# Attention and FFN in one kernel: v of four loads by SyncE's queue with a cast on GpSimd, and five more transposes by DMA

## The chip, the cores and the metric

The kernel runs on one core of one Trainium2 chip. The metric is the device time of one execution in microseconds. The engines are named as in the profile: PE (TensorE), DVE (VectorE), ACT (ScalarE), POOL (GpSimd) and SP (SyncE, which issues DMAs only).

## The reference

Attention with a bias by bucket of distance, followed by a two-layer FFN on the heads put side by side. Batch 8, 8 heads, 576 positions, head dimension 64; FFN 512 to 2048 to 512. All inputs and the output are float32.

```python
scores = scale * np.matmul(q, k.transpose(0, 1, 3, 2))
scores = scores + bias.transpose(2, 0, 1)[None, :, :, :]      # bias_table[bucket(|i - j|)]
attn = np.exp(scores - np.max(scores, axis=-1, keepdims=True))
attn = attn / (np.sum(attn, axis=-1, keepdims=True) + 1e-09)
attn_out = np.matmul(attn, v)
x = attn_out.transpose(0, 2, 1, 3).reshape(B * S, H * D)
h = x @ w_in
out = np.maximum(0.01 * h, h) @ w_out
```

## The kernel before

The work is cut into 32 items, `items[n] = (b, p)`: batch b and pair p of heads (2p and 2p+1), four pairs to a batch. Item n is called pair n below, counted from 0. The order of the instructions on each engine is written out by hand; nothing is moved by a scheduler, and each engine and each DMA queue works in that order.

For each pair the kernel turns q and k so that the head dimension lies on the partitions (`transpose_q`, `transpose_k`, both done in the loop of the pair before). Up to pair 8 PE turns them, twelve small products per operand into PSUM (L275), and ACT or DVE copies the result out (L290, L294). From pair 9 on (`by_dma`) DVE first gathers the rows of both heads in a tile `pr` (`pair_rows`, L257), SP issues a DMA transpose of it into a tile `tu` (`turn_by_dma`, L265), and DVE copies from `tu` to `qt` and `kt`. `turn_ahead(n)` decides in which loop that is done: for the pairs up to 10 two loops ahead, later three.

`qk_mm` forms the scores in PSUM (L312, L315, L316 and, into the two banks `ps_q`, L305), `exp` writes the exponentials to `at` by ACT (L325, L328, L332), `band` multiplies a band of them by the exponential of the bias on DVE (L348). `av_tails` and `av` multiply with v (L361, L372); v has a column of ones, so the sum of the weights comes with it. DVE takes the reciprocal and writes `opair` (L375, L376). The banks of `av` and of `ps_q` are the same two, so L305 waits until `opair` is written. `x_transposes` then turns `opair` into `xT`: by PE and a copy (L394, L395), or for pairs that `x_by_dma` names by a DMA transpose that SP issues (L387).

The FFN works on blocks of 512 tokens as soon as the batches they need are finished: `ffn_in` (L420) and `leaky` write the hidden block `gt` (two buffers), `ffn_out` (L447) reads it. Its pieces are put between the steps of attention; what remains comes at the end (`moe_rest`).

Loads: q, k and v come in float32 and are cast to bf16 by the DMA itself, on POOL's queue: `load_qk`, `load_v_head`, `load_v_part` (one DMA per chunk of 128 positions, pieces of one head's 64 numbers), `load_v_tail` for the last 64 positions; the weights too (`load_w_in`, `load_w_out`, two halves each). q, k and v of a batch lie in one of two buffers (`qn`, `kn`, `vn`, by b % 2). Batch 0, half of q and k of batch 1 and the rest are issued ahead of the loop; `loads(n)`, called first in the loop of pair n through `begin(n)`, issues the others. In it a copy of one number of `opair` of pair n - 2 into `tick` holds POOL's queue back until that pair is done. SP's queue carries the bias tables `hk` at the start, then the DMA transposes and the stores of the output.

Of the kernel before, what the change touches and what calls it, by code (L numbers as in the profile page):

```python
# [10 lines left out]
FP32 = mybir.dt.float32  # L11
BF16 = mybir.dt.bfloat16
# [25 lines left out]
def kernel(  # L38
# [10 lines left out]
    nc = tc.nc  # L49

    B, H, S, D = q.shape
# [4 lines left out]
    P = 128  # L56
    n_pairs = H // 2
    NJ = S // P
# [3 lines left out]
    TT = 512  # L62
    n_tt = NT // TT
    n_fc = DF // P
# [11 lines left out]
    gt_pool = ctx.enter_context(tc.tile_pool(name="gt", bufs=2))  # L76
# [17 lines left out]
    NBUF = 2  # L94
# [4 lines left out]
    vn = [per.tile([P, NJ, H, D + 1], BF16, name=f"vn{i}") for i in range(NBUF)]  # L99
# [9 lines left out]
    def load_qk(b, h0, h1):  # L109
        i = b % NBUF  # L110
        for src, dst in ((q, qn[i]), (k, kn[i])):
            nc.gpsimd.dma_start(  # L112
                out=dst[0:RQ, h0:h1, :, :].rearrange("r h c d -> r h (c d)"),
                in_=src[b, h0:h1, :, :].rearrange("h (r c) d -> r h (c d)", c=NC),
            )

    def load_v_part(b, chunks, h0=0, h1=H):
        for c in chunks:
            nc.gpsimd.dma_start(  # L119
                out=vn[b % NBUF][:, c, h0:h1, 0:D],  # L120
                in_=v[b, h0:h1, c * P : (c + 1) * P, :].rearrange("h s d -> s h d"),
            )

    def load_v_head(b, h):
# [2 lines left out]
            in_=v[b, h, 0 : NJ * P, :].rearrange("(c s) d -> s c d", s=P),  # L127
        )

    def load_v_tail(b):  # L130
        for e in range(2):
            nc.gpsimd.dma_start(
                out=v4[b % NBUF][e * SL : (e + 1) * SL, :, 0:D],
                in_=v[b, e::2, NJ * P : S, :].rearrange("h s d -> s h d"),
            )

    def clear_v(eng, i):
        eng.memset(v4[i][:, :, D : D + 1], 1.0)
        eng.memset(vn[i][:, :, :, D : D + 1], 1.0)
# [39 lines left out]
    for j, (u, lo, w, m) in enumerate(groups):  # L179
        copy = nc.scalar.copy if j % 3 == 2 else nc.vector.tensor_copy  # L180
        copy(out=ub[:, C0 + lo : C0 + lo + m * w].rearrange("h (m w) -> h m w", w=w),
             in_=e8[:, u : u + m].unsqueeze(2).to_broadcast([H, m, w]))
    row = ub[:, :]
    nc.vector.tensor_copy(
        out=ub[:, C0 - BAND + 1 : C0],
        in_=bass.AP(tensor=row.tensor, offset=row.offset + C0 + BAND - 1,
                    ap=[list(row.ap[0]), [-1, BAND - 1]]),
# [3 lines left out]
    def load_hk(h0, h1):  # L191
        nc.sync.dma_start(
            out=hk[:, h0:h1, :],
            in_=bass.AP(tensor=udr, offset=h0 * UW, ap=[[1, P], [UW, h1 - h0], [1, BW]]),
        )

    def load_hk4(p0, p1):
        for e in range(2):
            nc.sync.dma_start(
                out=hk4[e * SL : (e + 1) * SL, p0:p1, :],  # L200
                in_=bass.AP(tensor=udr, offset=(2 * p0 + e) * UW + SL + P,
                            ap=[[1, SL], [2 * UW, p1 - p0], [1, P + SL]]),
            )
# [3 lines left out]
    load_hk(2, 4)  # L207
    load_hk4(1, n_pairs)
    load_hk(4, H)

    def mirrored(t, lo, hi):

        w = t.shape[-1]
        v = t[..., w - hi : w - lo]
        ap = [list(d) for d in v.ap]
        ap[-1][0] = -1
        return bass.AP(tensor=v.tensor, offset=v.offset + hi - lo - 1, ap=ap)
# [8 lines left out]
    load_v_head(0, 2)  # L226
    load_v_head(0, 3)
    load_qk(1, 0, H // 2)
    load_v_part(0, range(NJ), 4, H)
    clear_v(nc.gpsimd, 1)  # L230
    load_qk(1, H // 2, H)

    def load_w_in(half):
        o = slice(half * (DF // 2), (half + 1) * (DF // 2))
        nc.gpsimd.dma_start(out=w_in_sb[:, :, o], in_=moe_w_in[:, o].rearrange("(c p) f -> p c f", p=P))

    def load_w_out(half):
        n = n_fc // 2
        nc.gpsimd.dma_start(
            out=w_out_sb[:, half * n : (half + 1) * n, :],  # L240
            in_=moe_w_out[half * n * P : (half + 1) * n * P, :].rearrange("(f p) e -> p f e", p=P),
        )
# [3 lines left out]
    qts, kts, ops_ = {}, {}, {}  # L246
    N = len(items)
# [10 lines left out]
                                  in_=src[b % NBUF][0:RQ, 2 * p : 2 * p + 2, :, :].rearrange("r e c d -> r c e d"))  # L258

    def by_dma(n):  # L260
        return n > 2 * n_pairs

    def turn_by_dma(n):
        t = turned[n] = tu_pool.tile([P, 2 * NC, RQ], BF16, name="tu")
# [2 lines left out]
    def turned_pair(n, j):  # L267

        if by_dma(n):
            return turned[n][:, j * NC : (j + 1) * NC, :].rearrange("p c r -> p r c")  # L270
        ps = ps_m_pool.tile([P, 8 * P], BF16, name="ps_t", tag="m")
        b, p = items[n]
        for c in range(NC):
            for e in range(2):
                nc.tensor.transpose(ps[e * D : (e + 1) * D, c * RQ : (c + 1) * RQ],  # L275
                                    in_=(qn, kn)[j][b % NBUF][0:RQ, 2 * p + e, c, :],
                                    identity=ident[0:RQ, 0:RQ])
        return ps[:, 0:S].rearrange("p (c r) -> p r c", c=NC)
# [98 lines left out]
                                in1=rcp.to_broadcast([P, NJ + 1, D]), op=ALU.mult)  # L377

    def x_by_dma(n):
        return n_pairs + 2 <= n < N - 1 and n != 2 * n_pairs - 1  # L380

    def x_transposes(n):
        b, p = items[n]
        opair = ops_[n]
        w = (NJ + 1) * P
        if x_by_dma(n):
            nc.sync.dma_start_transpose(  # L387
                out=xT[p][:, b * S : b * S + w].rearrange("p (i t) -> p i t", t=P),
                in_=opair.rearrange("p i d -> p (i d)"),
            )  # L390
            return
        ps = ps_m_pool.tile([P, 8 * P], BF16, name="ps_tx", tag="m")
        for ic in range(NJ + 1):
            nc.tensor.transpose(ps[:, ic * P : (ic + 1) * P], in_=opair[:, ic, :], identity=ident)  # L394
        nc.vector.tensor_copy(out=xT[p][:, b * S : (b + 1) * S], in_=ps[:, 0:S])  # L395


    gts = {}
    rest = {"on": False, "turn": 0}

    def bank(name):

        if rest["on"]:
            turn = rest["turn"] = (rest["turn"] + 1) % 6
            if turn % 3 == 0:
                return ps_o_pool.tile([P, 512], FP32, name=name, tag=f"o{turn // 3}")
            if turn % 3 == 1:
                return ps_s_pool.tile([P, 512], FP32, name=name, tag="ps_s")
        return ps_m_pool.tile([P, 512], FP32, name=name, tag="m")

    def ffn_in(T, f, spare=None):
        if f == 0:
            gts[T] = gt_pool.tile([P, n_fc, TT], BF16, name="gt")
        t0 = T * TT
        if spare is None:
            pm = bank("pm1")
        else:
            pm = ps_o_pool.tile([P, 512], FP32, name="pm1", tag=f"o{spare}")
        for c in range(n_cc):
            nc.tensor.matmul(pm, lhsT=w_in_sb[:, c, f * P : (f + 1) * P], rhs=xT[c][:, t0 : t0 + TT],  # L420
                             start=(c == 0), stop=(c == n_cc - 1))
        return pm
# [61 lines left out]
    def step(kind):  # L484
        T, s = made[kind], at_piece[kind]
        at_piece[kind] = (s + 1) % n_fc
        if at_piece[kind] == 0:
            made[kind] += 1
        return T, s
# [5 lines left out]
    def piece_in(spare=None):  # L495
        T, s = step("in")
        leaky(T, s, ffn_in(T, s, spare))
# [107 lines left out]
    tick = per.tile([1, 1], BF16, name="tick")  # L605

    def loads(n):

        b, p = items[n]
        if n == 0:  # L610
            load_w_in(0)
            load_v_part(1, range(NJ))
            load_v_tail(1)
            load_w_in(1)
            load_w_out(0)
        elif n == 2:
            load_qk(2, 0, H // 2)
            load_w_out(1)
        if b < 1 or p < 1 or b > B - 2:
            return  # L620
        nc.gpsimd.tensor_copy(out=tick, in_=ops_[n - 2][0:1, 0, 0:1])  # L621
        if p == 1:
            load_qk(b + 1, H // 2, H)
            load_v_part(b + 1, (0,))
        elif p == 2:
            load_v_part(b + 1, (1, 2, 3))
        else:
            load_v_tail(b + 1)
            if b + 2 < B:
                load_qk(b + 2, 0, H // 2)  # L630

    def begin(n):
        loads(n)
        if by_dma(n + 1):
            turn_ahead(n)

    def turn_ahead(n):
        for m in range(n + 2, min(n + AHEAD + 1, N)):
            if by_dma(m) and m - (AHEAD if m > 2 * n_pairs + 2 else 2) == n:
                pair_rows(m)  # L640
                turn_by_dma(m)
# [47 lines left out]
    n = n_pairs  # L689
# [24 lines left out]
    for n in range(n_pairs + 1, N + 1):  # L714
        live = n < N
        more = n + 1 < N
        if x_by_dma(n - 2):
            finished(n - 2)
# [30 lines left out]
        if not x_by_dma(n - 1):  # L749
            finished(n - 1)  # L750
# [5 lines left out]
        if room["only"]:  # L756
            exp(n, 3, ps_b)
            moe(2)
            exp(n, 4, ps_c)
            score(n, 5)  # L760
            T, f = step("in")
            room["left"] -= 1

            def last_bands():
                band(n, 5)
                band(n, 4)

            leaky(T, f, ffn_in(T, f), True, last_bands)
            moe(room["left"])
            continue  # L770
# [44 lines left out]
```

## Time and profile before

| | us |
|---|---|
| median of 3 runs | 378.06 (377.69 to 379.08) |
| the profiled execution | 378.04 |
| its span, from the first to the last instruction | 376.3 |
| PE busy | 366.1 |
| ACT busy | 239.9 |
| DVE busy | 199.1 |
| POOL busy | 77.3 |

Busy time is the time in which an engine had an instruction in work. A row of the profile's groups gives the line, the engine, the operation, what is written and read, the shape and the count, then the busy us, the mean ns of one, and the idle time of the engine just before with what ended it. In a timeline the first number is the start in us from the beginning of the span and the second the duration; instructions of one kind that follow each other are merged. DMA rows give the count, the size of one and the us from issue to landing.

### The profile page before, as it was taken

What the parts mean: (1) busy time and instruction counts of PE and PEld (TensorE: products, weight loads), DVE (VectorE), ACT (ScalarE), POOL (GpSimd) and SP (SyncE); (2) the same over time, 40 slices, a digit from 0 to 9 for tenths busy, and PEclk for the clock granted to TensorE, in tenths of its full rate; (3) what the DMA queues carried; (4) which work ended last, traced back from release to release, by engine and by line L of the source; (5) the groups of instructions that cost most, each with busy time, mean ns of one, the idle gap of its engine ahead of it and who ended that gap; (6) DMA issues with size and microseconds to landing.
All of it is one profiled execution on the core that took longest, in us unless ns stands there. A gap on an engine that the chain in (4) does not pass through costs nothing.

```text
span 376.3 us, 8737 instructions
## 1 busy us (share of the span) xinstructions
PE 366.1 (97%) x3604; PEld 186.7 (50%) x3604; DVE 199.1 (53%) x502; ACT 239.9 (64%) x376; POOL 77.3 (21%) x118
## 2 busy tenths in 40 slices
PE   7879999999999999999999999999999999999996
PEld 3455555554555555555545545555555544444442
DVE  3678577777657666666755666655553300200221
ACT  5998886568856787777866666767777255055000
POOL 8763422333023303330323033100000000000000
PEclk9999999999999999999999999999999999999999
DMA  8999999998599959997998399453111000110212
GB/s 104 189 194 186 206 199 120 181 179 121 77 119 157 145 85 123 151 152 91 142 118 132 72 124 127 74 79 77 47 47 47 28 30 0 59 54 0 82 60 84
DMA packets 104351, 40.06 MB, mean 106 GB/s; under 512 B 83184, under 2 KB 98808, under 8 KB 104312
## 3 DMA queue, kind: packets, MB, share of 16 engines
q0 software_dynamic: 53696, 18.36, 47.2%
q1 hardware_dynamic: 50472, 21.02, 31.7%
q8 instruction: 28, 0.46, 0.5%
q10 hardware_dynamic: 144, 0.13, 0.1%
q14 instruction: 11, 0.09, 0.1%
HBM read 37.68 MB, written 9.45 MB: 125 GB/s over the span
## 4 chain that ended last, share of the span: by engine, by line
PE 89%; DMA 5%; POOL 2%; DVE 2%; ACT 1%; issue 1%; DVEq 0%; ACTq 0%; POOLq 0%
PE pm L447 34%; PE pm L420 32%; PE ps_o L372 10%; PE ps_s L312 8%; DMA vn<-in_v_dram 3%; PE ps_s L315 2%; DMA v<-in_v_dram 1%; PE ps_o L361 1%; PE ps_q L305 1%; DVE opair L376 1%; PE ps_tx L394 1%; PE ps_t L275 1%; ACT at L325 1%; POOL kn L112 1%; POOL qn L112 0%
## 5 line engine op out<-in xcount | busy, mean ns | idle before, releaser
L420 PE MATMUL pm<-xT,w_in_sb 128*128 128x512 bf16 x576 | 138.4, 379 | 0.1
L433 ACT ACTIVATE gt<-pm 128x512 bf16<-128x512 f32 x138 | 82.5, 603 | 86.2 <-PE pm L420 85.7
L447 PE MATMUL pm<-w_out_sb,gt 128*128 128x512 bf16 x576 | 132.5, 379 | 0.0
L325 ACT ACTIVATE at<-ps_s 128x1024 bf16<-128x1024 f32 x128 | 124.2, 1028 | 8.2 <-PE ps_s L312 8.1
L348 DVE TENSOR_TENSOR at<-at,hk 128x768 bf16<-128x768 bf16 (+3 forms) x160 | 71.0, 453 | 32.7 <-ACT at L328 19.9
L447 PEld LDWEIGHTS <-gt 128*128 128x128 bf16 x576 | 53.0, 98 | 60.6
L420 PEld LDWEIGHTS <-w_in_sb 128*128 128x128 bf16 x576 | 52.0, 98 | 54.8 <-issue 0.7
L465 DVE COPY y<-pm 128x512 f32<-128x512 f32 x33 | 22.8, 691 | 76.6 <-PE pm L447 76.6
L372 PE MATMUL ps_o<-vn,at 128*128 128x65 bf16 x1280 | 49.8, 194 | 0.4 <-DMA vn<-in_v_dram 0.4
L372 PEld LDWEIGHTS <-at 128*128 128x128 bf16 x1280 | 44.7, 97 | 9.5 <-issue 1.2
L312 PE MATMUL ps_s<-qt,kt 64*128 64x512 bf16 x256 | 40.1, 381 | 3.5 <-ACT at L325 3.0
L375 DVE RECIPROCAL rcp<-ps_o 128x5 f32<-128x5 f32 x64 | 12.3, 192 | 45.1 <-PE ps_o L372 45.1
L376 DVE TENSOR_TENSOR opair<-ps_o,rcp 128x320 bf16<-128x320 f32 x64 | 31.5, 492 | 3.3
L119 POOL DMA_DIRECT2D vn<-in_v_dram x32 | 29.6, 931 | 10.0 <-PE ps_s L312 5.6
L621 POOL COPY tick<-opair 1x1 bf16<-1x1 bf16 x18 | 4.7, 263 | 130.8 <-DVE opair L376 130.8
L312 PEld LDWEIGHTS <-kt 64*128 64x128 bf16 x256 | 8.4, 94 | 29.0 <-issue 21.5
L332 ACT ACTIVATE at<-ps_s 128x576 bf16<-128x576 f32 x32 | 21.8, 681 | 0.2 <-PE ps_s L316 0.2
L328 ACT ACTIVATE at<-ps_q 128x256 bf16<-128x256 f32 x64 | 21.5, 402 | 0.3 <-PE ps_q L305 0.2
L457 ACT COPY y<-pm 128x256 f32<-128x256 f32 x1 | 0.4, 372 | 27.5 <-DVE y L457 27.5
L294 DVE COPY kt<-tu 128x576 bf16<-128x576 bf16 x23 | 15.5, 674 | 0.0
L290 DVE COPY qt<-tu 128x576 bf16<-128x576 bf16 x23 | 15.0, 650 | 0.4 <-DMA tu<-pr 0.4
L112 POOL DMA_DIRECT2D qn<-in_q_dram x18 | 14.1, 782 | 4.2 <-PE ps_t L275 1.3
(57 smaller groups left out, 175.0 us busy)
## 6 DMA issues: line engine op xcount, KB each, us to landing
out_dram<-y SPq DMA_DIRECT2D x35, 256.0 KB, 2.3
qn<-in_q_dram POOLq DMA_DIRECT2D x14, 288.0 KB, 5.9
kn<-in_k_dram POOLq DMA_DIRECT2D x14, 288.0 KB, 7.1
vn<-in_v_dram POOLq DMA_DIRECT2D x28, 128.0 KB, 5.2
w_in_sb<-in_moe_w_in_dram POOLq DMA_DIRECT2D x2, 1024.0 KB, 12.9
w_out_sb<-in_moe_w_out_dram POOLq DMA_DIRECT2D x2, 1024.0 KB, 15.9
qn<-in_q_dram POOLq DMA_DIRECT2D x4, 144.0 KB, 4.3
kn<-in_k_dram POOLq DMA_DIRECT2D x4, 144.0 KB, 4.6
```

What stands on the lines that cost most here:

```text
L119: nc.gpsimd.dma_start(out=vn[b % NBUF][:, c, h0:h1, 0:D], in_=v[b, h0:h1, c * P : (c + 1) * P, :].rearrange("h s d -> s h d"),)
L312: nc.tensor.matmul(ps[:, e, :], lhsT=kt[r, u * P : (u + 1) * P], rhs=qt[r, 0:512], start=True, stop=True)
L325: nc.scalar.activation(at[:, :, u, 0:512], ps, AF.Exp, scale=scale)
L328: nc.scalar.activation(at[:, e, :, 512:S], ps[e][:, 0 : NJ * SL].rearrange("p (c i) -> p c i", i=SL), AF.Exp, scale=scale)
L332: nc.scalar.activation(at4[:, 0:S], ps.rearrange("p e i -> p (e i)")[:, 0:S], AF.Exp, scale=scale)
L348: nc.vector.tensor_tensor(out=o, in0=o, in1=m, op=ALU.mult)
L372: nc.tensor.matmul(ps[:, ic, :], lhsT=at[:, o : o + P], rhs=vn[b % NBUF][:, c, 2 * p + e, :], start=False, stop=(ic == NJ and c == NJ - 1))
L376: nc.vector.tensor_tensor(out=opair[:, :, e * D : (e + 1) * D], in0=ps[:, :, 0:D], in1=rcp.to_broadcast([P, NJ + 1, D]), op=ALU.mult)
L420: nc.tensor.matmul(pm, lhsT=w_in_sb[:, c, f * P : (f + 1) * P], rhs=xT[c][:, t0 : t0 + TT], start=(c == 0), stop=(c == n_cc - 1))
L433: nc.scalar.activation(g, pm, AF.Prelu, bias=0.0, scale=1.0, alpha=0.01)
L447: nc.tensor.matmul(pm, lhsT=gt[:, f, ts * P : (ts + 1) * P], rhs=w_out_sb[:, f, :], start=(f == 0), stop=(f == n_fc - 1))
L465: nc.vector.tensor_copy(out=y, in_=pm)
```

## The change

`stage`, a float32 tile that shares its two buffers with `gt`, takes v as it is by SP's queue (`stage_v`), and POOL casts it into `vn` (`cast_v`). This replaces the casting DMAs of POOL's queue for heads 4 to 7 of batch 0, for batch 1 and for batch 2 (in two halves, in the loops of pairs 5 and 6). For batch 1 it is done in the loop of pair 3; a copy of one number by DVE into `stage` holds SP's DMAs until `opair` of pair 1 is there, and `load_w_out(0)`, the first half of `load_qk(2)` and `load_w_out(1)` are issued behind the cast. For batch 2 POOL's one-number copy goes into `stage` instead of `tick`; the cast stands in the loop of pair 7.

`by_dma` begins at pair 7 instead of 9. By `turn_ahead`, pair 7's rows are gathered and turned in the loop of pair 5 behind its first band product, pair 8's at the start of the loop of pair 6. Where the next pair is turned by DMA, `band(n, 0)` stands ahead of `transpose_q(n + 1)`, which now holds for the loops of pairs 6 and 7 too. `x_by_dma` begins at pair 5 instead of 6.

```diff
+    stage = gt_pool.tile([P, 2 * NJ, H, D], FP32, name="stage", tag="gt")
+
+    def stage_v(b, chunks, h0=0, h1=H):
+        for c in chunks:
+            nc.sync.dma_start(
+                out=stage[:, c, h0:h1, :],
+                in_=v[b, h0:h1, c * P : (c + 1) * P, :].rearrange("h s d -> s h d"),
+            )
+
+    def cast_v(b, h0=0, h1=H):
+        for c in range(NJ):
+            nc.gpsimd.tensor_copy(out=vn[b % NBUF][:, c, h0:h1, 0:D], in_=stage[:, c, h0:h1, :])
...
     load_hk4(1, n_pairs)
     load_hk(4, H)
+    stage_v(0, range(NJ), 4, H)
...
     load_qk(1, 0, H // 2)
-    load_v_part(0, range(NJ), 4, H)
     clear_v(nc.gpsimd, 1)
     load_qk(1, H // 2, H)
+    cast_v(0, 4, H)
...
     def by_dma(n):
-        return n > 2 * n_pairs
+        return n > 2 * n_pairs - 2
...
     def x_by_dma(n):
-        return n_pairs + 2 <= n < N - 1 and n != 2 * n_pairs - 1
+        return n_pairs + 1 <= n < N - 1 and n != 2 * n_pairs - 1
...
-            gts[T] = gt_pool.tile([P, n_fc, TT], BF16, name="gt")
+            gts[T] = gt_pool.tile([P, n_fc, TT], BF16, name="gt", tag="gt")
...
         if n == 0:
             load_w_in(0)
-            load_v_part(1, range(NJ))
             load_v_tail(1)
             load_w_in(1)
+        elif n == 3:
+            nc.vector.tensor_copy(out=stage[0:1, 0, 0, 0:1], in_=ops_[n - 2][0:1, 0, 0:1])
+            stage_v(1, range(NJ))
+            cast_v(1)
             load_w_out(0)
-        elif n == 2:
             load_qk(2, 0, H // 2)
             load_w_out(1)
         if b < 1 or p < 1 or b > B - 2:
             return
-        nc.gpsimd.tensor_copy(out=tick, in_=ops_[n - 2][0:1, 0, 0:1])
+        done = ops_[n - 2][0:1, 0, 0:1]
+        if b == 1 and p < 3:
+            nc.gpsimd.tensor_copy(out=stage[0:1, 2 * p - 2, 0, 0:1], in_=done)
+            stage_v(b + 1, (2 * p - 2, 2 * p - 1))
+        else:
+            nc.gpsimd.tensor_copy(out=tick, in_=done)
         if p == 1:
             load_qk(b + 1, H // 2, H)
+        if p == 1 and b > 1:
             load_v_part(b + 1, (0,))
-        elif p == 2:
+        elif p == 2 and b > 1:
             load_v_part(b + 1, (1, 2, 3))
-        else:
+        elif p == 3:
+            if b == 1:
+                cast_v(b + 1)
             load_v_tail(b + 1)
```

## The prediction

> **What bounds the kernel now.** I read the page first, then busy time by stretch, then the chain of work that ended last, then DVE, POOL and the DMA landings around the pairs that change.
>
> ```profile
> span 376.3 us, 8737 instructions
> PE 366.1 (97%) x3604; PEld 186.7 (50%) x3604; DVE 199.1 (53%) x502; ACT 239.9 (64%) x376; POOL 77.3 (21%) x118
> DMA  8999999998599959997998399453111000110212
> ```
> ```profile
> 20.00:30.00 10.00, 8.42 (x179) 5.84 (x180) 7.49 (x21) 9.33 (x14) 6.35 (x9) 1.00 1.48 192
> 40.00:50.00 10.00, 10.00 (x150) 6.00 (x147) 7.07 (x18) 8.45 (x13) 4.08 (x6) 1.00 1.26 205
> 50.00:60.00 10.00, 10.00 (x150) 6.05 (x150) 7.75 (x20) 8.03 (x13) 2.96 (x5) 1.00 2.09 169
> ```
>
> The stretch rows give busy us of PE, PEld, DVE, ACT, POOL, then clock, DMA share and GB/s. PE is busy 366.1 of 376.3 us. In the first 30 us ACT leads (9.33 of 10 us against PE's 8.42); from 40 us on PE has no gap, so PE work that goes away there is worth its full time, provided nothing PE waits for comes late. The DMA row is the warning: nearly all nines for the first 40% of the span. The loads of the first three batches and the weights form one unbroken backlog, and the change moves things inside it. The profiled execution took 378.04 us, 1.74 more than its span and 0.02 from the median 378.06; sums are made against 378.04. About 0.5% (1.9 us) is what a measurement of this kernel can tell from no change.
>
> **What leaves PE.** The chain of waits, in order of time (start, us, what):
>
> ```profile
> 49.22 0.38 PE ps_t L275 x12
> 51.17 0.38 PE ps_t L275 x12
> 51.55 0.54 PE ps_s L312 x4
> 52.09 0.19 PE ps_q L305 x8
> 52.28 0.39 PE ps_tx L394 x5
> 57.90 0.38 PE ps_t L275 x12
> 59.86 0.38 PE ps_t L275 x12
> ```
>
> q and k of pairs 7 and 8 (counted from 0) are the four groups of twelve transposes, the output of pair 5 the group of five, all on the chain: 4 x 0.38 + 0.39 = 1.91 us. The order of the FFN's pieces doesn't depend on these flags, so nothing else of PE's program changes. **If nothing came late: 378.04 - 1.91 = 376.13.**
>
> **What DVE gives back.** Each turned pair costs two `pair_rows` copies on DVE, put at the start of pair 6 (for pair 8) and behind the first band product of pair 5 (for pair 7).
>
> ```profile
> L257 DVE COPY pr<-kn 96x768 bf16<-96x768 bf16 x1 | 0.3, 348 | 0.0
> PEld L305 <- DVE opair L376: 0.4, 2, 0.2
> 42.53 0.19 DVE L375 RECIPROCAL rcp<-ps_o 128x5 f32<-128x5 f32 x1 [0.24 <-PE ps_o L372]
> ```
> ```profile
> 48.18 0.68 DVE L431 TENSOR_TENSOR gt<-low,pm 128x512 bf16<-128x512 bf16 x1
> 49.26 0.20 DVE L375 RECIPROCAL rcp<-ps_o 128x5 f32<-128x5 f32 x1 [0.39 <-PE ps_o L372]
> 49.55 0.49 DVE L376 TENSOR_TENSOR opair<-ps_o,rcp 128x320 bf16<-128x320 f32 x1
> 49.96 0.75 DVE L290 COPY qt<-ps_t 128x576 bf16<-128x576 bf16 x1
> 50.63 0.41 DVE L348 TENSOR_TENSOR at<-at,hk 128x512 bf16<-128x512 bf16 x1
> 51.21 0.20 DVE L375 RECIPROCAL rcp<-ps_o 128x5 f32<-128x5 f32 x1 [0.17 <-PE ps_o L372]
> ```
>
> The wait row shows PE's `ps_q` products waiting, in both these pairs, for the `opair` of the head before (it empties their bank): no slack there. Two copies take about 0.62 us (0.35 each, overlapping slightly); in pair 5 DVE has 0.24 us idle ahead of the reciprocal, so 0.62 - 0.24 = 0.38 us reaches PE. In pair 6 the same 0.62 falls into 0.39 us idle; besides, the k transposes that covered the evacuation are gone: PE has only the 0.54 us of L312 between `av` and `ps_q`, and the evacuation takes about 0.2 + 0.49 + 0.17 = 0.86. I take 0.32 for both together. Bounds: 0 to 0.7 each. Pair 7 keeps an FFN piece at that place, 0. **Floor: 376.13 + 0.38 + 0.32 = 376.8.** Casts, slot and gate below are counted apart.
>
> **The step that decides: k of batch 2.** `pair_rows(8)` reads q and k of heads 0 to 3 of batch 2. Before, they were read on PE at 57.90. Now DVE reaches them at 48.18 + 0.68 = 48.86 and stands in order: behind it wait the evacuation of pair 5, the band products and the copy of qt. When did k land?
>
> ```profile
> 21.82 0.75 POOL L235 DMA_DIRECT2D w_in_sb<-in_moe_w_in_dram  x1 [1.72 <-DMA qn<-in_q_dram]
> 34.16 0.89 POOL L239 DMA_DIRECT2D w_out_sb<-in_moe_w_out_dram  x1 [4.22 <-DMA w_in_sb<-in_moe_w_in_dram]
> 36.91 0.67 POOL L112 DMA_DIRECT2D kn<-in_k_dram  x1 [0.35 <-DMA vn<-in_v_dram]
> ```
> ```profile
> w_in_sb<-in_moe_w_in_dram POOLq DMA_DIRECT2D x1, 1024.0 KB, 12.1
> kn<-in_k_dram POOLq DMA_DIRECT2D x1, 288.0 KB, 14.1
> vn<-in_v_dram POOLq DMA_DIRECT2D x4, 128.0 KB, 11.9
> ```
>
> Issued at 36.91, 14.1 us to landing: 51.0. That is already 2.1 us too late for 48.86, so the change must bring it forward. What moves it:
> - v off POOL's queue: 512 x 4 + 1024 x 4 = 6144 pieces leave it and go to SP's queue, same pieces, fp32 instead of bf16.
>
> ```profile
> DMA packets 2978, 0.49 MB, mean 165 GB/s; under 512 B 2924, under 2 KB 2924, under 8 KB 2977
> DMA packets 2003, 0.73 MB, mean 243 GB/s; under 512 B 1875, under 2 KB 1881, under 8 KB 2002
> ```
>
>  The first row is v alone (30 to 33 us): about 975 small packets per us, so 6.3 us of DMA. The nearest row of 256-byte packets on SP's queue is the second (67 to 70 us, transposes): 625 per us, 9.8 us. Uncast copies may as well be cheaper, down to half. I take the same 6.3, a shift of 0 (-3.1 to +3.5).
> - POOL waits ahead of `load_w_in(0)` for the half v of batch 0 to land and its four casts; before, it issued at 21.82. v's half was landing until 26.96 (below), so I put it at 28. The gap on POOL's queue is partly filled by v of batch 1 on SP's: +0.5 (0 to 2).
> - `load_w_out(0)`, and q and k behind it, wait for v of batch 1: gate on DVE at about 24.8, four issues, some 11.9 us as before, casts: 37 to 41 instead of 34.16. POOL's queue still holds w_in's second half then: 0 (0 to 2).
> - New beside it on SP's queue: two chunks of v of batch 2 and the turn of pair 7, 2048 + 1152 pieces, 3.3 us at 975 per us. A third of it ahead of k: +1.0 (0 to 3.3).
>
> So k lands at 51.0 + 0.5 + 1.0 = 52.5. From there DVE needs the k copy 0.35, evacuation 0.7, band 0.41, qt 0.65, evacuation 0.7: 2.8 us to `ps_q`, 55.3 against 51.92 before (+3.4; the earlier savings and losses are swallowed by the wait). Then 0.39 + 2 x 0.38 = 1.15 is still saved. **Sum: 378.04 + 3.4 - 1.15 = 380.3**; in general 378.04 + (landing - 50.3).
>
> The Trainium skill (DMA: Bandwidth & Descriptors, Issuing engines are not separate DMA queues) says that DMAs from SP, ACT and GpSimd run on the same 16 DMA engines and interleave, so that a second issuer saves sequencer time only. By that rule the shift of the first item is 0 and the sum stays 380.3; it speaks against the hope of 376. The shift of 0 itself was taken from the packet counts.
>
> **Small parts.**
>
> ```profile
> 26.96 0.67 PE L372 MATMUL ps_o<-vn,at 128*128 128x65 bf16 x17 [0.43 <-DMA vn<-in_v_dram]
> masks.py:197 POOL MEMSET ident<- 128x128 bf16 x1 | 0.2, 231 | 0.0
> L799 POOL MEMSET const-float32-0.0<- 128x1 f32 x1 | 0.1, 98 | 0.2 <-issue 0.2
> 7.66 0.41 SPq L192 DMA_DIRECT2D hk<-u_row  x1
> 11.78 0.67 SPq L192 DMA_DIRECT2D hk<-u_row  x1
> DMA to landing us min/median/max: 3.3/4.0/8.1
> ```
>
> No row shows a cast on POOL. From its memsets, (231 - 98) / 127 = 1.0 ns per element: 0.36 us for 256, 0.62 for 512; 4 x 0.36 + 8 x 0.62 = 6.4 us in place of twelve v issues at some 0.9. POOL is busy 21%, so only its order counts. v of batch 0: PE waited 0.43 us for it; without that wait -0.43, with the last cast behind a landing at 27 some +0.8. SP pays per issue 0.41 us for 256 pieces and 0.67 for 512, by that slope 1.2 for 1024; behind the stage loads stand the turns of pairs 7 and 8 and the output transpose of pair 5. w_in's first half landed at 33.9, first used at 34.67; if its issue slips to 28, PE may wait 0 to 4 us, swallowed by the later wait up to 3.4. The gate on DVE is one small copy of an `opair` that is there: 0.1, in the ACT-led stretch. The slot that `stage` takes from gt is free again in pair 7's loads; the second token block starts after pair 7's output: 0, and if v of batch 2 came 10 us late, a wait of that.
>
> **Rivals.**
> 1. *All in time, no loss.* If uncast pieces cost half (-3.1), k lands by 48.9 and v's 0.43 goes too: 376.8 - 0.43 = 376.4 with both give-backs, 375.7 with neither, **376.1** in the middle. For: 1.91 us of PE work is gone for certain, and 6144 pieces are out of POOL's queue. Against: 51.0 in an unbroken backlog, and two added waits of POOL. Chance 0.26.
> 2. *v of batch 1 starves* beside w_in's big packets, POOL stands behind its cast, and w_out, q and k are issued at 41 or later, behind an empty queue: k at 57, **384.7**. Decides when v of batch 1 lands after 40. Chance 0.17.
> 3. *The turns come late.* Pair 8's stands behind two chunks of v; with the longest landing of the rows, 8.1 us, plus 2 us of issue, about 59 against a need at 58: 1 to 3 us on top of the floor, **379**. Chance 0.07.
> 4. *Casts block DVE.* A two-input product (L348) waits for one cast in each of three bursts: 0.36 + 0.62 + 0.62 = 1.6 on the floor: **378.4**. No row shows a POOL compute beside DVE. Chance 0.05. The Trainium skill (SBUF — State Buffer, SBUF: two separate sides) has this rule: one port pair is locked for a whole instruction by a GpSimd operation or by a DVE operation with two SBUF inputs, and the other blocks; no run here shows it yet.
>
> **How the numbers follow.** Forecast 380.3, chance 0.45, with k at 50 to 54.5, 377.7 to 382.3. Of it 0.17 lies within 0.5% (below 379.9), 0.28 above. Rival 1 gives 0.17 faster (give-backs mostly hidden, below 376.1) and 0.09 same, rival 2 0.17 slower, rivals 3 and 4 0.05 same and 0.07 slower. Together: faster 0.17, same 0.31, slower 0.52. The range from 375.8 to 386.0 leaves out the last of both ends.
>
> **What would show it.** Right: PE 1.9 us less busy, 53 fewer PE instructions; DVE idle 2 to 4 us at L257 in pair 6, released by the DMA of kn, PE then idle at L305 for `opair`; w_out, q and k issued after 37. Wrong: no idle time at L257 (rival 1); POOL's first cast of batch 1 ending after 41 (rival 2); DVE idle at L290 on tu (rival 3); L348 longer beside casts (rival 4).

## The result, and the profile after

The changed kernel takes 397.77 us in the median of 6 runs (395.17 to 401.54), the kernel before 377.78 beside it. The ratio of the two, with the one slow run of 401.54 us left out, is 1.0505, interval 1.0463 to 1.0548. The forecast was 380.3 with a range to 386.0; the change costs 20.0 us where 2.3 were expected. The profiled execution took 395.67 us with a span of 393.9, so 17.6 us more than the span before. It is that difference which the rows explain.

The page of the changed kernel, span, busy time and the slices of PE, granted clock and DMA:

```profile
span 393.9 us, 8604 instructions
PE 365.5 (93%) x3497; PEld 187.0 (47%) x3551; DVE 200.6 (51%) x506; ACT 240.1 (61%) x376; POOL 72.6 (18%) x118
PE   7859960999999999999999999999999999999995
PEclk9996995799999999999999999999999999999999
DMA  9999999869966975999499939943111100110112
```

PE's weight loads fell from 3604 to 3551: the 53 transposes are gone. PE's busy time did not fall by their 1.9 us, and the clock row says why: it shows two dips, where the same work takes longer. The second of them, the 7th slice of PE, is a hole. The stretches give both places (busy us of PE, PEld, DVE, ACT, POOL, then clock, DMA share, GB/s):

```profile
20.00:30.00 10.00, 6.15 (x123) 4.28 (x123) 5.51 (x15) 7.45 (x11) 2.24 (x5) 0.94 1.02 179
30.00:40.00 10.00, 9.72 (x139) 6.26 (x137) 7.07 (x19) 7.24 (x10) 5.47 (x9) 0.72 1.15 206
60.00:70.00 10.00, 1.81 (x11) 0.82 (x12) 3.06 (x6) 0.00 (x0) 1.89 (x4) 0.50 1.29 185
```

From 60 to 70 us PE is busy 1.81 us and ACT not at all, while DMA moves 185 GB/s: everybody waits for a transfer. The waits of PE and DVE name it (engine, line, releaser: total us, times, longest):

```profile
PE ps_q L319 <- DVE opair L390: 12.1, 2, 11.7
PE ps_o L386 <- POOL vn L141: 2.8, 2, 2.2
DVE qt L304 <- DMA tu<-pr: 10.3, 1, 10.3
DVE pr L271 <- DMA kn<-in_k_dram: 1.4, 1, 1.4
```

And the chain of work that ended last, in order of time (start, us, what):

```profile
47.30 19.54 DMA tu<-pr
66.87 0.64 DVE qt L304
67.64 0.50 DVE opair L390
68.19 0.39 PE ps_q L319 x7
```

PE stands 11.7 us at the `ps_q` products of pair 6, because the `opair` that empties their bank is queued on DVE behind the copy of pair 7's q (`qt`, L304) out of the tile in which the DMA transpose lays its turned q and k, and that turn took 19.54 us. The k of batch 2, the forecast's deciding wait, shows as 1.4 us on DVE and 0.43 us on PE.

Landmarks on PE's timeline tell how much each wait carries to the end. First the kernel before, then the changed one, the same products in each: the first of `av` in the loop of pair 5, `ps_q` in the loop of pair 6, then both in the loop of pair 7. Ahead of them, in the changed kernel, stand the two waits for v of batch 0.

```profile
39.50 0.31 PE L361 MATMUL ps_o<-v,at 64*128 64x65 bf16 x10
...
51.92 0.35 PE L305 MATMUL ps_q<-qt,kt 64*128 64x64 bf16 x8
...
56.88 0.31 PE L361 MATMUL ps_o<-v,at 64*128 64x65 bf16 x10
...
61.58 0.28 PE L305 MATMUL ps_q<-qt,kt 64*128 64x64 bf16 x8
```
```profile
28.65 0.19 PE L386 MATMUL ps_o<-vn,at 128*128 128x65 bf16 x1 [2.20 <-POOL vn L141]
29.43 1.10 PE L386 MATMUL ps_o<-vn,at 128*128 128x65 bf16 x17 [0.59 <-POOL vn L141]
...
43.95 0.32 PE L375 MATMUL ps_o<-v,at 64*128 64x65 bf16 x10
...
56.32 0.20 PE L319 MATMUL ps_q<-qt,kt 64*128 64x64 bf16 x1 [0.43 <-DVE opair L390]
68.19 0.39 PE L319 MATMUL ps_q<-qt,kt 64*128 64x64 bf16 x7 [11.67 <-DVE opair L390]
...
75.04 0.31 PE L375 MATMUL ps_o<-v,at 64*128 64x65 bf16 x10
...
78.77 0.28 PE L319 MATMUL ps_q<-qt,kt 64*128 64x64 bf16 x8
```

PE is 4.45 us behind in pair 5 (v of batch 0 late by 2.20 and 0.59, then half clock), 4.40 at `ps_q` of pair 6, 16.1 when the wait of 11.67 is over, 18.2 at `av` of pair 7's loop and 17.2 at its `ps_q`; the span ends 17.6 later. So **11.7 us come from the turn of pair 7, 4.4 from the stretch before, 2.1 from half clock behind the wait (2.45, less the 0.39 of pair 5's transposes), and the stretch that has lost pair 8's transposes takes 1.0 off.** Of that 1.0 the rows of the transposes give 0.76; the 0.4 us that the span gains behind the last landmark were not traced.

Why does a turn take 19.5 us? Two rows of SP's own queue (start, us to issue, instruction), and the packets moved in two windows, 54 to 58 us and 30 to 31 us (packets, MB, time as a share of 16 engines; q0 is POOL's queue, q1 is SP's; the last row is SP's queue alone):

```profile
42.54 1.43 SPq L134 DMA_DIRECT2D stage<-in_v_dram  x2
47.30 10.24 SPq L279 DMA_TRANSPOSE tu<-pr  x1
```
```profile
q0 software_dynamic: 609, 0.61, 90.4%
q1 hardware_dynamic: 607, 0.16, 29.7%
```
```profile
q1 hardware_dynamic: 985, 0.25, 110.5%
```

Alone, SP's queue moved 985 small packets per us. Beside POOL's backlog of q, k and w_out it got one packet for each of POOL's, 607 against 609 in 4 us, or 152 per us, and POOL's are about 1 KB each (0.61 MB in 609). Between 20 and 24 us it was 773 against 775, 193 per us. Ahead of the turn in that queue stand two chunks of v, 2048 pieces, then its own 1152. At 152 to 193 per us these 3200 take 16.6 to 21.1 us; from v's issue at 42.54 to the turn's landing at 66.84 it was 24.3 us. The difference lies at the start: from 42 to 46 us SP's queue moved no packet at all, and from 46 to 47 only 45. From 46.4, when they begin in earnest, to the landing it is 20.4 us, or 157 per us for the 3200, which is the pace of one for one (in the last of these microseconds the queue already moves pieces of the next two chunks of v). Why nearly 4 us pass between the issue and the first packets, the record doesn't show.

### The profile page after: what moved, and what is told of

It is laid out like the page before. It is cut to its first block, busy times and chain, and to the rows that moved or that the text cites. A ratio compares the mean times of both kernels' runs of the same rounds, so it can differ in the third digit from the quotient of the medians.

```text
span 393.9 us, 8604 instructions
## 1 busy us (share of the span) xinstructions
PE 365.5 (93%) x3497; PEld 187.0 (47%) x3551; DVE 200.6 (51%) x506; ACT 240.1 (61%) x376; POOL 72.6 (18%) x118
## 4 chain that ended last, share of the span: by engine, by line
PE 78%; DMA 13%; SPq 2%; DVE 2%; ACT 1%; issue 1%; another core or an unknown queue 1%; POOL 0%; DVEq 0%; POOLq 0%
PE pm L461 31%; PE pm L434 28%; PE ps_o L386 9%; PE ps_s L326 7%; DMA stage<-in_v_dram 5%; DMA tu<-pr 5%; DMA kn<-in_k_dram 2%; PE ps_s L329 1%; PE ps_o L375 1%; SPq L134 1%; PE ps_q L319 1%; DMA u_row<-ub 1%; SPq L212 1%; DMA tabT<-in_bias_table_dram 1%
## 5 line engine op out<-in xcount | busy, mean ns | idle before, releaser
L461 PE MATMUL pm<-w_out_sb,gt 128*128 128x512 bf16 x556 | 130.8, 379 | 1.0
L461 PEld LDWEIGHTS <-gt 128*128 128x128 bf16 x576 | 53.0, 98 | 60.6
L434 PEld LDWEIGHTS <-w_in_sb 128*128 128x128 bf16 x576 | 52.4, 99 | 56.1 <-issue 3.2
L386 PE MATMUL ps_o<-vn,at 128*128 128x65 bf16 x1280 | 50.9, 195 | 2.8 <-POOL vn L141 2.8
L386 PEld LDWEIGHTS <-at 128*128 128x128 bf16 x1280 | 45.6, 99 | 12.2 <-issue 3.9
L326 PEld LDWEIGHTS <-kt 64*128 64x128 bf16 x256 | 8.4, 94 | 28.8 <-issue 20.8
L304 DVE COPY qt<-tu 128x576 bf16<-128x576 bf16 x25 | 16.2, 650 | 10.3 <-DMA tu<-pr 10.3
L319 PE MATMUL ps_q<-qt,kt 64*128 64x64 bf16 x256 | 9.6, 193 | 12.2 <-DVE opair L390 12.1
L119 POOL DMA_DIRECT2D vn<-in_v_dram x20 | 19.0, 957 | 2.9 <-PE ps_o L386 1.7
L319 PEld LDWEIGHTS <-kt 64*128 64x128 bf16 x256 | 7.8, 96 | 19.8 <-DVE opair L390 13.1
## 6 DMA issues: line engine op xcount, KB each, us to landing
w_out_sb<-in_moe_w_out_dram POOLq DMA_DIRECT2D x2, 1024.0 KB, 16.6
```

The source lines that it names most:

```text
L319: nc.tensor.matmul(ps[e][:, c * SL : (c + 1) * SL], lhsT=kt[r, c * P : (c + 1) * P], rhs=qt[r, 512:S], start=True, stop=True)
L326: nc.tensor.matmul(ps[:, e, :], lhsT=kt[r, u * P : (u + 1) * P], rhs=qt[r, 0:512], start=True, stop=True)
L386: nc.tensor.matmul(ps[:, ic, :], lhsT=at[:, o : o + P], rhs=vn[b % NBUF][:, c, 2 * p + e, :], start=False, stop=(ic == NJ and c == NJ - 1))
L461: nc.tensor.matmul(pm, lhsT=gt[:, f, ts * P : (ts + 1) * P], rhs=w_out_sb[:, f, :], start=(f == 0), stop=(f == n_fc - 1))
```

## The experiments

The theory: the turn of pair 7 is late because SP's queue gets packets one for one with POOL's, and v of batch 2 stands ahead of it; the clock falls behind the waits and adds a few us. Rivals: the k wait of the forecast is the main loss; transposes by DMA are slow by themselves; one half of the change alone does the harm.

**The two halves apart.** First the turns without the staging, from the kernel before:

```
     def by_dma(n):
-        return n > 2 * n_pairs
+        return n > 2 * n_pairs - 2
...
     def x_by_dma(n):
-        return n_pairs + 2 <= n < N - 1 and n != 2 * n_pairs - 1
+        return n_pairs + 1 <= n < N - 1 and n != 2 * n_pairs - 1
```

> The kernel before with the two conditions of the change alone (q and k of pairs 7 and 8, output of pair 5 by DMA); all loads as before. Theory 'shared turn' (while POOL's queue is backed up, SP's queue moves one packet for each of its packets, and what delayed pair 7's turn were the 2048 pieces of v of batch 2 ahead of it): pair 7's turn now stands first on SP's queue, 1152 packets at about 190 per us, 6 to 7 us from issue to landing, no wait of DVE for it over 1 us; what is left is the wait for k of batch 2, which lands at 51.0 before against 48.9 needed, so 378 to 381. Theory 'slow transposes' (a DMA transpose beside POOL's loads takes 19 us whatever stands ahead): DVE waits some 9 us for pair 7's turn, 387 to 392.

Measured 384.68 us, 1.0185 times the kernel before (1.0147 to 1.0223), so +7.0. DVE's timeline (start, us, instruction, wait and releaser):

```profile
51.96 0.35 DVE L257 COPY pr<-kn 96x768 bf16<-96x768 bf16 x1 [2.84 <-DMA kn<-in_k_dram]
55.45 0.64 DVE L290 COPY qt<-tu 128x576 bf16<-128x576 bf16 x1 [2.10 <-DMA tu<-pr]
```

Here is the forecast's wait, at its line and of its size: k of batch 2 lands at about 51.95 and DVE stands 2.84 us. But the turn of pair 7 is late behind it too, with no v on SP's queue: issued at 42.48, it took 12.95 us to land, and pair 8's took 12.6. PE waits 2.01 and 3.50 us at L305. Neither forecast for this run had its number. The 6 to 7 us of the theory count the 1152 packets alone, at 190 per us. Here, too, the queue's first packets came only at 46.4, 3.9 us after the issue, and the 9.0 us that are left make 128 per us.

Then the staging without the turns, which is the changed kernel with both conditions put back:

> The changed kernel with the two conditions of the transposes as in the kernel before: only the loads of v go another way. Theory 'shared turn' and theory 'slow transposes' agree here: no early turn, so the 10 to 12 us in pair 6 go; PE still waits 2.8 us for the cast v of batch 0 at 28 us and runs some us at a lower granted clock after it. 381 to 384. If the staging by itself cost the most, it would stay above 390.

Measured 384.14 us, 1.0164 (1.0136 to 1.0193), +6.5. PE's timeline shows a third of it:

```profile
46.47 0.68 PE L386 MATMUL ps_o<-vn,at 128*128 128x65 bf16 x17 [2.09 <-POOL vn L141]
```

v of batch 1 is late behind its cast; PE's weight loads wait for w_in, 2.2 us at about 39 us, and the clock is low for one stretch of 3.4 us. The halves cost 7.0 and 6.5, together 20.0: 6.5 us exist only when both are there. Both put their work on SP's queue.

**Order or share on SP's queue.** Two kernels take v of batch 2 out of the turn's way. One loads it by POOL's queue as before:

```
-        if b == 1 and p < 3:
-            nc.gpsimd.tensor_copy(out=stage[0:1, 2 * p - 2, 0, 0:1], in_=done)
-            stage_v(b + 1, (2 * p - 2, 2 * p - 1))
-        else:
-            nc.gpsimd.tensor_copy(out=tick, in_=done)
+        nc.gpsimd.tensor_copy(out=tick, in_=done)
...
-        if p == 1 and b > 1:
+        if p == 1:
             load_v_part(b + 1, (0,))
...
-            if b == 1:
-                cast_v(b + 1)
```

> The changed kernel with v of batch 2 loaded by POOL's queue with its cast, as before; v of batches 0 and 1 still staged, pairs 7 and 8 still turned by DMA. Theory 'shared turn': pair 7's turn stands alone on SP's queue, 6 to 7 us to landing, so DVE no longer waits 10 us for it and PE's clock does not drop a second time: 382 to 386. Theory 'slow transposes': the 10 us stay, 394 to 399.

Measured 390.23, 1.0329 (1.0299 to 1.0358). The other has SP issue the same chunks behind the turn of the same loop:

```
-            stage_v(b + 1, (2 * p - 2, 2 * p - 1))
+            held.append((b + 1, (2 * p - 2, 2 * p - 1)))
...
             turn_ahead(n)
+            release()
```

(`release` issues what is held.)

> The changed kernel with one order changed: on SP's queue v of batch 2 is issued behind the turn of the same loop instead of ahead of it. Same bytes, same queues. Theory 'shared turn': pair 7's turn lands 6 to 7 us after its issue at 47, no wait there; pair 8's turn has 2048 pieces ahead of it and may be 0 to 5 us late: 383 to 389. Theory 'slow transposes' or one of total DMA load: unchanged, 395 to 399.

Measured 391.44, 1.0362 (1.0314 to 1.0411). DVE's timeline of the two, this order:

```profile
59.05 0.35 DVE L271 COPY pr<-kn 96x768 bf16<-96x768 bf16 x1 [2.96 <-DMA kn<-in_k_dram]
61.51 0.64 DVE L304 COPY qt<-tu 128x576 bf16<-128x576 bf16 x1 [1.08 <-DMA tu<-pr]
```
```profile
61.19 0.64 DVE L304 COPY qt<-tu 128x576 bf16<-128x576 bf16 x1 [2.07 <-DMA tu<-pr]
```

The wait of 10.27 us falls to 1.08 and 2.07, and both times lie between the forecasts. The turn, issued at 48.23 and 47.28, is copied 13.3 and 13.9 us later instead of 19.6. So v ahead of it made some 6 us, and some 13 are left with nothing ahead of it, as with the turns alone; the theory had 6 to 7 for this. The rival that a turn beside POOL's loads is slow by itself so has the larger part right, though not as a matter of transposing: v's plain pieces had the same 4 us ahead of their first packets and the same pace of one for one. In the changed kernel DVE was free for that copy at 56.6 (66.87 - 10.27), and a turn of 13.3 us issued at 47.30 lands at 60.6: by this estimate it would still be 4 us late without v.

k's wait grows from 1.42 to 2.96 us in the first kernel and 3.15 in the second; its copy starts at 59.05 and 57.73 instead of 55.21. Most of that is a later issue, at 43.83 and 42.88 instead of 40.78, because k stands on POOL's queue behind the cast of v of batch 1. Up to there these two programs are the changed kernel's own. The last of the four casts starts at 38.65 in the changed kernel's profile, at 41.71 and 40.75 in these two and at 45.80 in that of the staging alone, so the landing of v of batch 1 differs by microseconds between executions of the same instructions. A single microsecond between two of these profiles should not be read as an effect of the edit. Of the 8 to 9 us that DVE's wait for the turn loses, 7.5 and 6.3 come off the time.

**Packets or bytes.** If SP's queue is paced by the number and size of POOL's packets, it is faster without w_out's large ones beside it. The second half of w_out is issued one loop later:

```
             load_qk(2, 0, H // 2)
-            load_w_out(1)
...
             if b == 1:
+                load_w_out(1)
                 cast_v(b + 1)
```

> The changed kernel with the second half of w_out issued in the loop of pair 7, ahead of the cast of v of batch 2, instead of right behind q and k of batch 2. Theory 'shared turn' (one packet of SP's queue for each of POOL's while both are backed up): its 1024 packets no longer stand between 46 and 62 us, POOL's queue runs empty some 6 us earlier and SP's queue then moves at its own pace of 800 packets per us and more; pair 7's turn lands 5 to 7 us earlier than 66.9: 390 to 393. A theory of shared bandwidth (bytes, not packets) gives about the same bytes per us to SP's queue and at most 2 to 3 us: 394 to 396.

Measured 392.59, 1.0369 (1.0332 to 1.0406), 5.2 less than the changed kernel.

```profile
63.34 0.64 DVE L304 COPY qt<-tu 128x576 bf16<-128x576 bf16 x1 [3.96 <-DMA tu<-pr]
```

The turn was issued later, at 51.14 instead of 47.30, yet landed earlier: 12.2 us instead of 19.5. Counted from the issue of v ahead of it, at 44.57, it is 18.7 us instead of 24.3. In the same window, 54 to 58 us, POOL's queue now moves

```profile
q0 software_dynamic: 774, 0.57, 90.9%
q1 hardware_dynamic: 773, 0.19, 36.6%
```

The ratio is still one to one, at 193 per us instead of 152. This is the packets' account.

**The clock.** Products whose result nobody reads keep PE busy in the two waits:

```
+            if n == 3:
+                fill(12)
             av(n - 1, 0)
...
+            if n == 6:
+                fill(52)
+            ps_c = qk_mm(n, 4)
```

> The changed kernel with products of zeros that nobody reads put where PE waits: 12 of them ahead of the first weighted sums of pair 2 (where it waited 2.8 us for the cast v of batch 0) and 52 ahead of the last scores of pair 6 (where it waited some 12 us for pair 7's turn); 216 ns each, so they end before the waits do. They do no work of the reference. Theory 'clock' (each long wait costs PE a stretch at half the granted clock behind it: 28.8 to 35.6 us and 59.5 to 73.2 us in the changed kernel's profile, some 5 to 6 us together): the waits stay, the clock stays at 1, 391 to 393. Rival 'waits alone' (the low clock is hidden by ACT, or costs nothing that later slack doesn't give back): 396 to 399.

Measured 394.57, 1.0438 (1.0402 to 1.0474), 3.2 less than the changed kernel in the medians and between the two forecasts. The granted clock of the changed kernel, then of this one:

```profile
core 0: 393.9 us, clock 0.974
```
```profile
core 0: 391.5 us, clock 1.000
```

The clock is full throughout. PE's and DVE's timelines show what that is worth:

```profile
56.79 11.40 PE L618 MATMUL ps_f<-junk 128*128 128x512 bf16 x51
68.12 0.29 PE L319 MATMUL ps_q<-qt,kt 64*128 64x64 bf16 x8
...
72.59 0.31 PE L375 MATMUL ps_o<-v,at 64*128 64x65 bf16 x10
```
```profile
63.98 0.65 DVE L304 COPY qt<-tu 128x576 bf16<-128x576 bf16 x1 [5.72 <-DMA tu<-pr]
```

`ps_q` starts at 68.12, as in the changed kernel (68.19), and the next `av` at 72.59 instead of 75.04: 2.45 us for the second dip, and 2.4 is what the span lost. The first dip brought nothing, since PE then waited 1.51 us for w_in. The turn landed 2.9 us earlier here, at 63.98, but the filling went on to 68.1, longer than the wait by then, and hid that. Nothing in this run says more about the turn.

**v of batch 0.** Half of it goes back to POOL's queue, without cast:

```
-    stage_v(0, range(NJ), 4, H)
...
+    load_v_part(0, range(NJ), 4, H)
...
-    cast_v(0, 4, H)
```

> The changed kernel with half of v of batch 0 loaded by POOL's queue with its cast, as before; v of batches 1 and 2 still staged, all turns as changed. Theory 'shared turn': the wait at 26 to 29 us and the low clock behind it go (4.5 us up to pair 5), the wait for pair 7's turn in pair 6 stays: 392 to 395. Rival (the backlog alone sets when pair 7's turn lands, at 67 us, whatever PE does before): PE comes earlier to the same wait, 396 to 398.

Measured 398.03, 1.0526 (1.0496 to 1.0556): no gain. v of batch 1 is late instead, PE waiting 2.19, 0.86 and 0.80 us for it, and DVE's wait for the turn stays, at 10.12 us. The rival had the number, but not the way: PE came to the wait later, not earlier (58.81 instead of 56.32), and the turn landed at 69.2, not at 67. That the backlog sets the end, whichever piece of v stands in it, fits this run but is not shown by it.

**Is there a version that gains?** The theory says yes if the turns come early and few. From the kernel before, pair 5's output by DMA and pair 7's turn alone, issued a loop earlier (by then q and k of batch 1 have long landed):

```
     def by_dma(n):
-        return n > 2 * n_pairs
+        return n > 2 * n_pairs or n == 2 * n_pairs - 1
...
     transpose_q(n + 1)
+    pair_rows(2 * n_pairs - 1)
+    turn_by_dma(2 * n_pairs - 1)
```

> The kernel before with the output of pair 5 and q and k of pair 7 by DMA, pair 8 still turned on PE, and pair 7's turn issued in the loop of pair 4, some 5 us earlier than in the change; all loads as before. If what hurt was only when the turns are issued and what stands before them: the turn is issued near 38 us and lands 11 to 12 us later, near 50, when DVE needs it; PE saves 2 x 0.38 + 0.39 = 1.15 us and gives back 0 to 0.5: 376.8 to 378. If a turn inside the backlog is late in any case: DVE waits 1 to 3 us in pair 6, 379 to 382.

Measured 381.97, 1.0096 (1.0062 to 1.0129). DVE's timeline:

```profile
50.76 0.64 DVE L290 COPY qt<-tu 128x576 bf16<-128x576 bf16 x1 [0.97 <-DMA tu<-pr]
71.89 0.65 DVE L290 COPY qt<-tu 128x576 bf16<-128x576 bf16 x1 [3.65 <-DMA tu<-pr]
```

Pair 7's turn, issued at 37.15, takes 13.6 us even there, its first packets at 41.1. And pair 9's turn, for which DVE waited 0.40 us before, is now late by 3.65 us. To see which part does this, the output of pair 5 alone:

```
     def x_by_dma(n):
-        return n_pairs + 2 <= n < N - 1 and n != 2 * n_pairs - 1
+        return n_pairs + 1 <= n < N - 1 and n != 2 * n_pairs - 1
```

> The kernel before with the output of pair 5 by DMA and nothing else: five products of PE less, 0.39 us of the chain, 640 packets more on SP's queue at 52 us. Theory (a turned output has some 25 us until the second token block reads it, so its landing does not matter): 0.2 to 0.5 us faster, 377.2 to 377.5. Rival (its packets push the next turn on the same queue, pair 9's, which DVE already waited 0.4 us for): no change or up to 1 us slower.

Measured 380.45 in 12 runs, 1.0047 (1.0025 to 1.0070): saving 0.39 us of PE costs 1.8 by the ratio and 2.5 in the medians, more than either forecast had. It is near the 0.5% that the prediction took for noise, but 1 lies outside the interval of the 12 runs.

```profile
72.30 0.65 DVE L290 COPY qt<-tu 128x576 bf16<-128x576 bf16 x1 [2.90 <-DMA tu<-pr]
```

One more transfer, of 0.39 us of PE work, and pair 9's turn (issued at 61.26) lands 11.0 us after its issue, where it took 8.7 in the kernel before (60.29 to 68.97). Outputs of pairs 4 and 5 by DMA:

> The kernel before with the outputs of pairs 4 and 5 by DMA and nothing else: ten products of PE less, 0.78 us of the chain, 1280 packets more on SP's queue between 43 and 56 us. Theory (landing does not matter): 0.5 to 0.9 us faster, 376.8 to 377.2. Rival (packets in the backlog push the loads of POOL's queue and pair 9's turn): 378 to 380.

Measured 381.59, 1.0110 (1.0069 to 1.0150), slower than both forecasts, with DVE waits for turns of 3.02 and 2.10 us. Last, both turn conditions without staging, and w_out's second half one loop later:

> The kernel before with all turns of the change and the second half of w_out issued one loop later, behind the other half of q and k of batch 2; v as before. Theory (while both queues are backed up each packet of POOL's queue lets one of SP's by, and k of batch 2 is behind w_in and the first half of w_out in any case): DVE still waits 2 to 3 us for k at about 51, pair 7's turn still takes 10 us or more, since q and k come in w_out's place: 381 to 385, near the 384.7 of the turns alone. If w_out's second half was what held k and the turn back: 377 to 379.

Measured 383.63, 1.0158 (1.0126 to 1.0190), about as the turns alone. k's wait falls to 1.23 us and pair 7's turn's to 1.01 (it still takes 12.0 us to land), but q of batch 2 is now waited for, 1.78 us. No version came under the kernel before.

## Why the prediction was wrong

**PE's work.** Right: 53 instructions left PE. The 1.91 us stayed invisible in its busy time, since the stretches at half clock lengthened the rest.

**k of batch 2.** Right in place, and nearly in size: DVE waits at the `pair_rows` line for k, 2.84 us with the turns alone, 2.96 with v of batch 2 on POOL's queue. The landing was forecast at 52.5 and came at 51.95 without staging and at 55.2 (issued 40.78, 14.4 us) with it. But it was not the step that decides: in the changed kernel it costs PE 0.43 us.

**The step that failed** is the item "two chunks of v of batch 2 and the turn of pair 7 ... a third of it ahead of k: +1.0". It asked only what SP's new packets do to k on POOL's queue, not what POOL's backlog does to SP's. Its 3200 packets were priced at 975 per us, the rate of v when that queue was alone, 3.3 us. Measured beside POOL's large packets: 152 to 193 per us while they moved, behind 3.9 us after v's issue in which SP's queue moved next to nothing; together 24.3 us, and the turn landed 19.54 us after its own issue. And the wait for that turn, by the copy of qt on DVE in pair 6 with `opair` behind it, had no term: the sum has the 0.65 us of the copy and takes the turn as landed. It was 10.27 us on DVE and 11.67 on PE. Rival 3 had the right queue and the right line (DVE idle on tu) but pair 8's turn and 1 to 3 us; rival 2 had the starving beside large packets, but on v of batch 1. Neither joined the two. The largest landing of the rows, 8.1 us, was taken as a bound, though no row had shown a turn inside the backlog of the first 60 us, where it takes 12 to 14 us even with nothing ahead of it on its queue. (The row leaves out pair 9's, which took 8.7 us before.) Rival 2's own mechanism is there as well: v of batch 1 landed just before 38.65 in the changed kernel's profile, short of the 40 that it names, and after 40 in four other kernels that have the same loads up to there.

**The first item, v off POOL's queue,** was a shift of 0, and the rates bear it out: 985 packets per us alone on SP's queue, 975 on POOL's. The same pieces cost the same. What the sum lacked is that they wait far longer when another queue is served in turn with them. The Trainium skill (DMA: Bandwidth & Descriptors, Queues, rings and completion order) says that each engine serves its rings round-robin by packets of several descriptors; 609 against 607 and 775 against 773 agree with turns of equal number. The Trainium skill's rule quoted in the prediction (DMA: Bandwidth & Descriptors, Issuing engines are not separate DMA queues), that a second issuer saves sequencer time only, agrees as well: 197 GB/s from both queues between 54 and 58 us, 249 from SP's alone between 30 and 31. It is milder than the case: here the second queue's small pieces lost.

**v of batch 0.** Forecast -0.43 to +0.8, measured 2.8 us in two waits. Its pieces went to SP's queue beside POOL's, at 773 packets against 775 between 20 and 24 us. With the first dip of the clock PE was 4.45 us behind by pair 5.

**The clock** had no term. The second dip cost 2.45 us, by the run that kept PE busy; the first lay mostly ahead of a wait for w_in.

**Casts.** Forecast 0.36 and 0.62 us, measured 0.40 and 0.62. Rival 4's mechanism is there in DVE's timeline behind the long wait, where POOL casts v of batch 2 from 68.02 to 69.76:

```profile
68.05 1.08 DVE L308 COPY kt<-tu 128x576 bf16<-128x576 bf16 x1
69.17 0.67 DVE L296 TENSOR_TENSOR kt<-kt,own 128x128 bf16<-128x128 bf16 x1
```

These take 0.65 and 0.22 us elsewhere, so 0.43 and 0.45 more. The Trainium skill's rule in the prediction (SBUF — State Buffer, SBUF: two separate sides) agrees for the product, 0.67 us beside a cast, whose two inputs lie in SBUF. The copy, with one input, was slowed as well. It is 0.9 us on DVE, beside 17.6 of the span.

**The give-backs on DVE** were about right. Between `av` in the loop of pair 5 and `ps_q` in that of pair 6, 12.42 us before and 12.37 after, 0.76 us of transposes are gone and 0.71 come back (forecast 0.38 + 0.32 = 0.70). That it fits is in part luck: 0.43 of the 0.71 are PE's wait at `ps_q` in pair 6, which has the wait for k in it.

**What was not taken apart.** Of the 6.5 us of interaction, how much is order and how much is share: the run with the turn first gains 6.3 and the one with w_out late 5.2, and in each other waits show. What part of it is the time before a queue's first packet was not tried either.

## What to carry to other kernels

When a transfer moves to another queue, price it at the rate that queue gets while the others are full, and count everything already queued ahead of it, then ask who stands in order behind its reader. Here a queue of 256-byte pieces beside one of kilobyte packets got a fraction of its own speed, and moving compute to DMA in the part of the span where DMA has no gap was a loss even for 0.4 us of work. A bound taken from rows of a calm stretch is no bound for a full one.

## What the runs showed of the hardware

- Two queues with work were served packet for packet, 775 to 773 and 609 to 607, with packets of about 0.7 and 1 KB on one and 256 bytes on the other. SP's rate fell from 985 packets per us to 152.
- Inside the backlog some 4 us passed from an issue on SP's idle queue to its first packets: 42.54 to 46.4 for v of batch 2, 42.48 to 46.4, 48.23 to 52.4 and 37.15 to 41.1 for pair 7's turn in three other kernels. Why is open.
- SP's issue itself takes longer there: 10.24 us for one transposing transfer behind two stage loads, against 1.7 to 3.1 us for the same turn in four kernels where it stands first. Why, and whether it adds to the landing, is open.
- The clock fell to half at 28.8 us, where PE's wait of 2.20 us ended; another of 0.59 followed. In the kernel with v of batch 2 on POOL's queue it fell at the end of a gap of 0.85 us, shortly behind one of 0.62. Its PE timeline shows two products taking 0.61 us, which take 0.39 at full clock:

```profile
21.13 0.61 PE L326 MATMUL ps_s<-qt,kt 64*128 64x512 bf16 x2 [0.85 <-ACT at L339]
```

  The records show half clock there from 21.1 to 24.5 us. The Trainium skill (TensorE: Matmul & The Clock Gate, Part 1: The HAM clock gate (the "warmup" mystery)) speaks of about 3.4 us of idle time ahead of the slow clock; the length of the dips agrees, the idle time ahead of them was shorter here. But the length of a gap doesn't decide it: in the kernel with w_out late the same gaps of 0.62 and 0.85 us, at 18.4 and 20.7 us, left the clock at 1.00. What exactly brings the dip on was not tried.
